# Pooled attention, a Sinkhorn-gated expert layer and a softplus layer on one core: softmax, gate, Sinkhorn, expert sums and pacing rewritten

## The chip, the cores and the metric

The kernel runs on one core of a Trainium2 chip. The metric is the device time of one execution in microseconds (us). The time before is 2142.21 us, the median of 3 runs.

## What is computed

The reference has three layers in a row, on 2304 tokens (4 batches of 576) of 512 features:

```
k_p, v_p = mean over groups of 8 tokens            # 72 keys and values a head
attn = softmax(q k_p^T / 8), divided by (sum + 1e-9);  x = attn v_p     # 8 heads of 64
P = exp(x w_gate - max over all);  8 times:        # P is 2304 x 8, Sinkhorn
    P /= P.sum(1) + 1e-9;  P /= P.sum(0) + 1e-9;  P *= 2304 / 8
x = sum over 8 experts e of P[:, e] * (relu(x w1[e]) w2[e])              # 1024 hidden
out = softplus(x w_in) w_out                       # 2048 hidden
```

## The kernel before, in words

**Precision.** Every large product is made of three matmuls on rounded parts (`three`, L451): high by high, high by low, low by high. ScalarE (ACT) rounds a tile to its high part, GpSimd (POOL) or VectorE (DVE) subtracts to get the low part.

**Order.** The order of the work is written by hand, engine by engine; each engine runs its own queue in that order. All loads and stores are issued by SP's queue, in order. The tokens are cut into three groups of 512, 896 and 896 (`PAIRS`). The 512 come first: the expert layer of group 0 runs while attention for the rest is still going on, in its gaps. Then come the expert layer of groups 1 and 2, then the softplus layer of groups 1, 2 and 0. An expert layer of a group is 32 sets (8 experts by 4 slices of 256 hidden units). A set has a `first` product (seven products of a Strassen-like scheme, `first_moe`, L518) and a `second` product (`second`, L581), one for every 128 tokens. `first` of set n+1 goes ahead of `second` of set n.

**Hooks.** After each of the seven products of `first`, and after each tile of `second`, `hook` (L721) is called: a slot. A set of group 0 has 7 + 4 = 11 slots. While attention is not done, every fourth slot issues one attention step (L724). After that each slot pops one entry of the list `side`; when that is empty, slots feed the conversion of the softplus weights from float64 (`from_float64`, L665).

**Attention steps.** There are 32 (4 batches, 2 halves of 288 tokens, 4 head pairs). Ten run ahead of the experts (L767), 22 in the slots. `attn_step` (L376) issues: the transposes of the next step's queries; the scores `s` into a PSUM bank, 96 tokens by 6 rows of 72 scores (`softmax`, L297); on DVE the negated maximum `mx`; the transposes of the step before (`turn_attn`); on ACT six exps, one per row of 72 with its own bias, each with a sum read out (L313); on DVE the sum plus 1e-9 and its reciprocal; on POOL the product with it (L321); then the mix with the values (`mix`, L336), whose result `px` ACT copies to `x0` or `xb`. With a half's fourth head pair, `mix` also stores `xb` and makes the gate's logits `pg` (L357): for each 96 tokens and each quarter of the features the 96 token columns are the weights and the 8 columns of `w_gate` are streamed, 12 matmuls of two instructions each. ACT copies them to `lt`. The last quarter of the features is what `mix` has just written. `pool_kv` sums keys and values over groups of 8 tokens on DVE.

**After attention.** `finish_attention` (L707) fills `side`: `to_tiles` stores `lt` to DRAM and loads it back as `prob` [128, 18, 8]; then the maximum; then eight times `sk_rows`, three empty slots, `sk_cols` (L638, L645), all on small tiles in SBUF except the column sums, which a matmul with ones puts into a bank `pc`; then `shares_to_raw`. The shares `prob` are not known when the first experts run: for group 0 the outputs of experts 0 to 3 (`RAW = 4`) are summed without shares, each in a tile of its own (`second`, L600), and `shares_to_raw` (L745) multiplies and adds them later, on DVE, 16 entries of `side`. From expert 4 on DVE multiplies the share in as it takes a tile out of PSUM (L610).

**Banks.** The 8 PSUM banks are one pool until attention is over; then 4 serve `first`, 3 (`y`) serve `second` and small things, 1 (`c`) serves the conversion and the softplus.

**Between groups.** `load_x` (L758) brings the next group's tokens; `t_sums` (L418) makes four sums of them, three on DVE and one on POOL; `splits` rounds seven tiles of them during the last `first` of a group. Weights go through one raw buffer each (`load_w`, L141) and are rounded by `prep_w1` and `prep_w2` (L177, L201); the load for a raw buffer is issued behind the preparation that empties it. In the last set of group 0 (set 31), whose `first` is followed by `second` of sets 30 and 31, `prep_w2` of set 31 and the load behind it are issued ahead of the seven products (L837).

Of the kernel before, what the change touches and what calls it, by code (L numbers as in the profile page):

```python
# [19 lines left out]
def attention_moe_softplus_kernel(  # L20
# [39 lines left out]
    OFF = (0, 512, 1408)  # L60
    LARGE = max(PAIRS)
    TP0 = PAIRS[0]
    RAW = 4

    cpool = ctx.enter_context(tc.tile_pool(name="const", bufs=1))
    xpool = ctx.enter_context(tc.tile_pool(name="x", bufs=14))
# [26 lines left out]
    row = cpool.tile([P, NT], F32, name="row")  # L93
    col = cpool.tile([P, E], F32, name="col")


    big = cpool.tile([P, 10], F32, name="big")
    rcpool = ctx.enter_context(tc.tile_pool(name="rconst", bufs=1, side="right"))
    lt = rcpool.tile([QP, 248], F32, name="lt")[:, :N // QP * E].rearrange("p (g e) -> p g e", e=E)
    nc.scalar.preload_act_table_set("natural_log_exp_and_others")  # L100


# [4 lines left out]
    def acc_of(i, t):  # L107
        return g_t[i][:, t * DM:(t + 1) * DM]

    def x_of(pair):  # L110
        return g_t[0][:, :KC * PAIRS[pair]].rearrange("p (c n) -> p c n", c=KC)

# [6 lines left out]
    lgd = dram.tile([N, E], F32, name="lgd")  # L119
    v1 = {}  # L120
    v2 = {}
    for u in range(NU2):
# [3 lines left out]

    phases = [("moe", 0), ("moe", 1), ("moe", 2), ("sp", 1), ("sp", 2), ("sp", 0)]
    acc_at = [1, 3, 2, 3, 2, 1]
    raw_at = [1, 0, 2, 3]
    sets = [  # L130
        (f, kind, pair, u)
        for f, (kind, pair) in enumerate(phases)
# [164 lines left out]
    def softmax(m):  # L297

        ps = bank("s")
        qT = q_t.pop(m)  # L300
        kb = kbd[kv_of(m) % NK]
        for j in range(JH):
            nc.tensor.matmul(ps[:QP, j * 2 * SP:(j + 1) * 2 * SP], qT[:, j * QP:(j + 1) * QP], kb)  # L303
        sv = ps[:QP, :G * SP].rearrange("p (g s) -> p g s", g=G)
        pool = at_e if m < AHEAD and m % 3 == 2 else at_p
        mx = at_p.tile([QP, G], F32, tag="mx", name="mx")
        ex = pool.tile([QP, G, SP], F32, tag="ex", name="ex")
        s1 = ps[:QP, G * SP:G * SP + G]
        nc.vector.tensor_reduce(mx, sv, axis=AX.X, op=ALU.max, negate=True)

        def exp():
            for g in range(G):
                nc.scalar.activation(  # L313
                    ex[:, g, :], sv[:, g, :], AF.Exp, bias=mx[:, g:g + 1], accum_out=s1[:, g:g + 1]
                )

        def divide():
            sm = at_p.tile([QP, G], F32, tag="sm", name="sm")
            nc.vector.tensor_scalar_add(s1, s1, 1e-9)
            nc.vector.reciprocal(sm, s1)  # L320
# [15 lines left out]
    def mix():  # L336
        m, aT = to_mix.pop(0)
        hb, hp = divmod(m, HP)
        vp = pooled[kv_of(m)][1]
        px = bank("px")  # L340
        for h in range(2):
            nc.tensor.matmul(px[h * D:(h + 1) * D, :W], vp[:, h, :], aT[:, h, :])  # L342

        t0 = hb * W
        here = max(0, min(W, TP0 - t0))
        x0 = x_of(0)
        if here < W and hp == 0:
            xb[hb] = at_p.tile([P, KC, W], F32, tag="xb", name="xb")
        if here:
            nc.scalar.activation(x0[:, hp, t0:t0 + here], px[:, :here], AF.Copy, scale=1.0 / POOL)  # L350
        if here < W:
            nc.scalar.activation(xb[hb][:, hp, :], px[:, :W], AF.Copy, scale=1.0 / POOL)
        if hp == HP - 1:
            if here < W:
                nc.sync.dma_start(xd[:, :, max(0, t0 - TP0):t0 + W - TP0], xb[hb][:, :, here:])
            pg = bank("pg")
            for j in range(JH):  # L357
                for c in range(KC):
                    o = j * QP
                    src = x0[:, c, t0 + o:t0 + o + QP] if here == W else xb[hb][:, c, o:o + QP]  # L360
                    nc.tensor.matmul(  # L361
                        pg[:QP, j * E:(j + 1) * E], src, wg[:, c, :], start=c == 0, stop=c == KC - 1
                    )
            nc.scalar.copy(lt[:, hb * JH:(hb + 1) * JH, :], pg[:QP, :JH * E].rearrange("p (j e) -> p j e", j=JH))


    pool_at = {}
# [213 lines left out]
    def second(n, i):  # L581
        f, kind, pair, u = sets[n]
        t = OFF[pair] // P + i
        py = bank("py")
        hh, hl = h_t[n]
        whi, wlo = w2_t[n]
        cs = slice(i * P, (i + 1) * P)
        for c in range(UC):
            three(py, (hh[:, c, cs], hl[:, c, cs]), (whi[:, c, :], wlo[:, c, :]), c == 0, c == UC - 1)
        a = acc_of(acc_at[f], i)  # L590
        if kind == "sp":
            if u == 0:
                nc.scalar.copy(a, py)
            else:
                nc.vector.tensor_tensor(a, py, a, op=ALU.add)
            if u == NU2 - 1:
                nc.sync.dma_start(out[t * P:(t + 1) * P, :], a)
            return
        e, first = u // UPE, u % UPE == 0
        if f == 0 and e < RAW:  # L600

            a = acc_of(raw_at[e], i)
# [14 lines left out]
        nc.scalar.copy(x_of(pair)[:, :, i * P:(i + 1) * P], pt)  # L617


    def to_tiles():  # L620
        nc.sync.dma_start(lgd.rearrange("(g p) e -> p g e", p=QP), lt)
        nc.sync.dma_start(prob, lgd.rearrange("(t p) e -> p t e", p=P))

    def sk_max():
        nc.vector.tensor_reduce(big[:, 0:1], prob, axis=AX.XY, op=ALU.max)
# [10 lines left out]
        nc.scalar.activation(prob, prob, AF.Exp, bias=big[:, 0:1])  # L636

    def sk_rows():  # L638
        nc.vector.tensor_reduce(row, prob, axis=AX.X, op=ALU.add)
        nc.vector.tensor_scalar_add(row, row, 1e-9)  # L640
        nc.vector.reciprocal(row, row)
        nc.vector.tensor_tensor(prob, prob, row.unsqueeze(2).to_broadcast([P, NT, E]), op=ALU.mult)
        nc.vector.tensor_reduce(col, prob.rearrange("p t e -> p e t"), axis=AX.X, op=ALU.add)

    def sk_cols():  # L645
        pc = bank("pc")
        nc.tensor.matmul(pc[:, :E], ones, col)
        nc.vector.tensor_scalar_add(col, pc[:, :E], 1e-9)
        nc.vector.reciprocal(col, col)
        nc.vector.tensor_scalar_mul(col, col, float(N // E))  # L650
        nc.vector.tensor_tensor(prob, prob, col.unsqueeze(1).to_broadcast([P, NT, E]), op=ALU.mult)

# [54 lines left out]
    def finish_attention():  # L707
        actx.close()
        gp = ctx.enter_context(tc.tile_pool(name="g23", bufs=1))
        for i in (2, 3):  # L710
            g_t[i] = gp.tile([P, GW], F32, name=f"g{i}")
        pools.append(ctx.enter_context(tc.tile_pool(name="tmp", bufs=2)))
        side.extend([to_tiles, None, None, None, None, None, sk_max, None, sk_max_t, None, sk_max_b])
# [7 lines left out]
    def hook(light=True):  # L721
        slot[0] += 1
        if attn_m[0] is not None:
            if slot[0] % 4 == 2:  # L724
                attn_step(attn_m[0], False)
                attn_m[0] += 1
                if attn_m[0] >= STEPS and not to_turn and not to_mix:
                    attn_m[0] = None
                    finish_attention()
# [14 lines left out]

    def shares_to_raw(experts):  # L745

        mul, stt = nc.vector.tensor_scalar_mul, nc.vector.scalar_tensor_tensor
        for i in range(TP0 // P):
            for e in experts:
                def add(i=i, e=e):  # L750
                    a, s = acc_of(1, i), prob[:, i, e:e + 1]
                    if e == 0:
                        mul(a, a, s)
                    else:
                        stt(a, acc_of(raw_at[e], i), s, a, op0=ALU.mult, op1=ALU.add)  # L755
                side.append(add)

    def load_x(pair):  # L758
        o = OFF[pair] - TP0
# [58 lines left out]
    for step, (what, n) in enumerate(todo):  # L818
# [4 lines left out]
        elif what == "first":  # L823
# [7 lines left out]
            if nxt is not None and nxt[0] != f:  # L831

                flush()
                if kind == "moe":
                    x = x_of(nxt[2])
                    to_split = splits(nxt[1], x, t_in(2, nxt[2]), on_pool=(2, 4) if nxt[1] == "moe" else (1, 3))
                if todo[step + 2][0] == "second":  # L837
                    prep_w2(n)
                    load_w(2, n + 1)
            elif kind == "sp" and u == 4 and f + 1 < len(phases):  # L840
                flush()
                to_split = splits("sp", x_of(phases[f + 1][1]), None, on_pool=(1, 3))
# [13 lines left out]
            if kind == "moe":  # L856

                pending.pop(0)()
                prep_w1(n + 1)
                load_w(1, n + 2)  # L860
            if todo[step + 1][0] != "second":
# [5 lines left out]
        else:  # L867
# [70 lines left out]
```

## Time and profile before

| what | value |
|---|---|
| median of 3 runs | 2142.21 us (2141.76 to 2143.05) |
| profiled execution, its own time | 2141.97 us |
| its span, first to last instruction | 2140.0 us |
| PE busy (matmul) | 2054.6 us, 96% |
| DVE, ACT, POOL busy | 67%, 41%, 59% |
| mean granted PE clock | 0.978 |

PE is TensorE's matmul row; its busy time counts every matmul from start to end and grows when the clock is low, so a busy PE need not be a fast one. The granted clock is 1.00 at 2.4 GHz and 0.50 at 1.2 GHz.

### The profile page before, as it was taken

Reading aid. Unit: us, or ns where it says so; the run is one execution under the profiler, and the core shown is the slowest. Engines: PE = TensorE matmul, PEld = TensorE weight load, DVE = VectorE, ACT = ScalarE, POOL = GpSimd, SP = SyncE. Lnnn points to the kernel's source line nnn. Section 1 sums busy time; section 2 is a strip of 40 time slices with the busy share of each in tenths; the row PEclk is TensorE's granted clock in tenths of the full one; section 3 lists DMA queues with packets and bytes.
Section 4 is the critical chain, followed back from the end, with each engine's and each line's share of the span. In section 5 each row is a group of like instructions: output and inputs, shape, how many; then the busy total and the mean of one; then the engine's idle time right before and its main releaser. Section 6 shows DMA issues by size and latency. Waiting matters only on the chain.

```text
span 2140.0 us, 28131 instructions
## 1 busy us (share of the span) xinstructions
PE 2054.6 (96%) x10411; PEld 1787.7 (84%) x10411; DVE 1437.1 (67%) x2453; ACT 867.1 (41%) x1921; POOL 1258.9 (59%) x1015
## 2 busy tenths in 40 slices
PE   7788989999799999999999999999999999999998
PEld 5677778888688888888887888888888888888897
DVE  5555388877667777777777776555555666767766
ACT  6655633333432222222234223222222355565565
POOL 4554477999655565555566565555555544544555
PEclk8798999999999999999999999999999999999999
DMA  6333222444222322222222222111112111121132
GB/s 174 91 102 95 64 81 89 128 126 155 74 89 83 110 83 89 89 86 77 89 89 80 83 89 70 60 58 56 56 59 60 60 60 50 60 84 60 50 114 79
DMA packets 132073, 179.19 MB, mean 84 GB/s; under 512 B 30816, under 2 KB 83040, under 8 KB 131936
## 3 DMA queue, kind: packets, MB, share of 16 engines
q1 hardware_dynamic: 131936, 177.40, 26.8%
q8 instruction: 81, 1.33, 0.3%
q14 instruction: 56, 0.46, 0.1%
HBM read 160.52 MB, written 16.85 MB: 83 GB/s over the span
## 4 chain that ended last, share of the span: by engine, by line
PE 81%; DVE 8%; ACT 6%; POOL 2%; issue 2%; DMA 1%; SPq 0%; ACTq 0%; DVEq 0%; POOLq 0%
PE py L454 40%; PE p L454 30%; PE ph L454 7%; ACT ex L313 2%; POOL w1lo L161 1%; PE pg L361 1%; DVE xlo L432 1%; PE s L303 1%; DVE c L485 1%; PE pa L332 1%; POOL w2lo L161 0%; DVE ln L492 0%; DVE c L490 0%; DVE g L755 0%; PE px L342 0%
## 5 line engine op out<-in xcount | busy, mean ns | idle before, releaser
L454 PE MATMUL py<-w2hi,hhi 128*128 128x512 f32 x1440 | 569.2, 395 | 7.4 <-DVE g L610 4.9
L454 PE MATMUL py<-w2lo,hhi 128*128 128x512 f32 x1440 | 564.1, 392 | 1.9 <-POOL w2lo L161 1.9
L454 PE MATMUL py<-w2hi,hlo 128*128 128x512 f32 x1440 | 563.5, 391 | 0.0
L161 POOL TENSOR_TENSOR w1lo<-w1raw,w1hi 128x512 fp32r<-128x512 f32 (+1 forms) x216 | 253.8, 1192 | 506.8 <-ACT w1hi L192 421.1
L454 PE MATMUL p<-xhi,w1hi 128*128 128x448 f32 (+1 forms) x1344 | 463.8, 345 | 31.2 <-DVE u L534 16.0
L454 PE MATMUL p<-xhi,w1lo 128*128 128x448 f32 (+1 forms) x1344 | 459.4, 342 | 2.6 <-POOL w1lo L161 2.6
L454 PE MATMUL p<-xlo,w1hi 128*128 128x448 f32 (+1 forms) x1344 | 460.2, 342 | 0.3
L610 DVE SCALAR_TENSOR_TENSOR g<-py,prob,g 128x512 f32<-128x512 f32 x498 | 372.7, 749 | 121.2 <-PE py L454 108.0
L469 ACT ACTIVATE hhi<-p 128x448 fp32r<-128x448 f32 (+1 forms) x384 | 179.7, 493 | 448.0 <-PE p L454 435.5
L454 PEld LDWEIGHTS py<-w2hi,hhi 128*128 128x128 f32 x1440 | 272.5, 189 | 65.5 <-DVE g L610 6.0
L161 POOL TENSOR_TENSOR w2lo<-w2raw,w2hi 128x1024 fp32r<-128x1024 f32 x120 | 289.1, 2409 | 61.6 <-ACT w2hi L205 56.3
L454 PEld LDWEIGHTS py<-w2hi,hlo 128*128 128x128 f32 x1440 | 272.0, 189 | 59.5
L454 PEld LDWEIGHTS py<-w2lo,hhi 128*128 128x128 f32 x1440 | 272.5, 189 | 52.3 <-POOL w2lo L161 2.2
L454 PEld LDWEIGHTS p<-xhi,w1hi 128*128 128x128 f32 x1344 | 259.6, 193 | 61.3 <-DVE u L534 17.3
L454 PEld LDWEIGHTS p<-xlo,w1hi 128*128 128x128 f32 x1344 | 259.7, 193 | 19.3 <-DVE xlo L432 0.9
L454 PEld LDWEIGHTS p<-xhi,w1lo 128*128 128x128 f32 x1344 | 259.7, 193 | 16.6 <-POOL w1lo L161 3.8
L536 ACT COPY za<-p 128x448 f32<-128x448 f32 (+1 forms) x96 | 46.0, 479 | 516.2 <-PE p L454 514.0
L161 POOL TENSOR_TENSOR w1lo<-sums,w1hi 128x1024 fp32r<-128x1024 f32 x96 | 230.5, 2401 | 0.0
L470 DVE SCALAR_TENSOR_TENSOR hlo<-p,hhi 128x448 fp32r<-128x448 f32 (+1 forms) x384 | 210.8, 550 | 27.1 <-ACT hhi L469 25.7
L534 DVE TENSOR_TENSOR za<-p,za 128x448 f32<-128x448 f32 (+1 forms) x96 | 53.2, 554 | 164.1 <-PE p L454 164.0
L497 POOL TENSOR_TENSOR hlo<-ln,hhi 128x448 fp32r<-128x448 f32 (+1 forms) x96 | 99.9, 1044 | 55.5 <-ACT hhi L496 52.9
L454 PE MATMUL ph<-xhi,w1hi 128*128 128x448 f32 (+1 forms) x384 | 130.1, 339 | 0.0
(117 smaller groups left out, 2779.5 us busy)
## 6 DMA issues: line engine op xcount, KB each, us to landing
w1raw<-in_moe_w_dram SPq DMA_DIRECT2D x96, 512.0 KB
w2raw<-in_moe_w_dram SPq DMA_DIRECT2D x96, 512.0 KB
w1raw<-v SPq DMA_DIRECT2D x24, 512.0 KB
w2raw<-v SPq DMA_DIRECT2D x24, 512.0 KB
f<-in_moe_w_in_dram SPq DMA_DIRECT2D x16, 512.0 KB
v<-dt SPq DMA_DIRECT2D x32, 256.0 KB
f<-in_moe_w_out_dram SPq DMA_DIRECT2D x16, 512.0 KB
kt<-in_k_dram SPq DMA_DIRECT2D x16, 288.0 KB
```

What stands on the lines that cost most here:

```text
L161: nc.gpsimd.tensor_tensor(o, a, b, op=ALU.subtract)
L303: nc.tensor.matmul(ps[:QP, j * 2 * SP:(j + 1) * 2 * SP], qT[:, j * QP:(j + 1) * QP], kb)
L313: nc.scalar.activation(ex[:, g, :], sv[:, g, :], AF.Exp, bias=mx[:, g:g + 1], accum_out=s1[:, g:g + 1])
L332: nc.tensor.transpose(pa[:SP, j * QP:(j + 1) * QP], ex[:, 2 * j + h, :], ident[:QP, :QP])
L361: nc.tensor.matmul(pg[:QP, j * E:(j + 1) * E], src, wg[:, c, :], start=c == 0, stop=c == KC - 1)
L454: nc.tensor.matmul(ps, lhs[a], rhs[b], start=first and i == 0, stop=last and i == 2, skip_group_check=goes_on,)
L469: nc.scalar.activation(hh, src, AF.Relu)
L470: nc.vector.scalar_tensor_tensor(hl, src, 0.0, hh.bitcast(F32), op0=ALU.max, op1=ALU.subtract)
L497: nc.gpsimd.tensor_tensor(hl, l, hh.bitcast(F32), op=ALU.subtract)
L534: add = lambda o, x, y: nc.vector.tensor_tensor(o, x, y, op=ALU.add)
L536: nc.scalar.copy(a, pa)
L610: nc.vector.scalar_tensor_tensor(a, py, prob[:, t, e:e + 1], a, op0=ALU.mult, op1=ALU.add)
```

## The change

1. **Softmax.** DVE subtracts the maximum from all 432 scores into `ex` in SBUF; one exp on ACT covers them; DVE sums `ex` over 72.
2. **Gate.** `w_gate`'s 8 columns are the weights; 288 token columns are streamed, 4 matmuls of two instructions a half. ACT copies 8 x 288 logits to `lg`, and each half's are stored to DRAM at once. `to_tiles` becomes one load; `to_prob` turns it with two PE transposes.
3. **Sinkhorn.** `row` and the column factors live in PSUM banks.
4. **Raw experts.** Five instead of four; `raw_of` packs them into the four accumulator tiles. Expert 0 is scaled on ACT, and two empty slots follow each product of the others.
5. **Pacing.** An attention step every fifth slot; two empty slots behind each of `t_sums`; `prep_w2` of set 31 and the load behind it are issued behind its seven products.

```diff
-    RAW = 4
+    RAW = 5
-        nc.vector.tensor_reduce(mx, sv, axis=AX.X, op=ALU.max, negate=True)
+        nc.vector.tensor_reduce(mx, sv, axis=AX.X, op=ALU.max)
+        nc.vector.tensor_tensor(ex, sv, mx.unsqueeze(2).to_broadcast([QP, G, SP]), op=ALU.subtract)
         def exp():
-            for g in range(G):
-                nc.scalar.activation(
-                    ex[:, g, :], sv[:, g, :], AF.Exp, bias=mx[:, g:g + 1], accum_out=s1[:, g:g + 1]
-                )
+            nc.scalar.activation(ex, ex, AF.Exp)
         def divide():
+            nc.vector.tensor_reduce(s1, ex, axis=AX.X, op=ALU.add)
...
-            for j in range(JH):
-                for c in range(KC):
...
-                    nc.tensor.matmul(
-                        pg[:QP, j * E:(j + 1) * E], src, wg[:, c, :], start=c == 0, stop=c == KC - 1
-                    )
-            nc.scalar.copy(lt[:, hb * JH:(hb + 1) * JH, :], pg[:QP, :JH * E].rearrange("p (j e) -> p j e", j=JH))
+            src = x0[:, :, t0:t0 + W] if here == W else xb[hb]
+            for c in range(KC):
+                nc.tensor.matmul(pg[:E, :W], wg[:, c, :], src[:, c, :], start=c == 0, stop=c == KC - 1)
+            lg = at_p.tile([E, W], F32, tag="lg", name="lg", bufs=1)
+            nc.scalar.copy(lg, pg[:E, :W])
+            half, o = divmod(t0, LT * P)
+            nc.sync.dma_start(lgd[half, :, o:o + W], lg)
...
     def sk_rows():
+        row = bank("row", "c")[:, :NT]
...
     def sk_cols():
         pc = bank("pc")
         nc.tensor.matmul(pc[:, :E], ones, col)
-        nc.vector.tensor_scalar_add(col, pc[:, :E], 1e-9)
-        nc.vector.reciprocal(col, col)
-        nc.vector.tensor_scalar_mul(col, col, float(N // E))
-        nc.vector.tensor_tensor(prob, prob, col.unsqueeze(1).to_broadcast([P, NT, E]), op=ALU.mult)
+        c = pc[:, :E]
+        nc.vector.tensor_scalar_add(c, c, 1e-9)
+        nc.vector.reciprocal(c, c)
+        nc.vector.tensor_scalar_mul(c, c, float(N // E))
+        nc.vector.tensor_tensor(prob, prob, c.unsqueeze(1).to_broadcast([P, NT, E]), op=ALU.mult)
...
-            if slot[0] % 4 == 2:
+            if slot[0] % 5 == 2:
...
-        for i in range(TP0 // P):
-            for e in experts:
+        for e in experts:
+            for i in range(TP0 // P):
                 def add(i=i, e=e):
                     a, s = acc_of(1, i), prob[:, i, e:e + 1]
                     if e == 0:
-                        mul(a, a, s)
+                        nc.scalar.activation(a, a, AF.Copy, scale=s)
                     else:
-                        stt(a, acc_of(raw_at[e], i), s, a, op0=ALU.mult, op1=ALU.add)
-                side.append(add)
+                        nc.vector.scalar_tensor_tensor(a, raw_of(e, i), s, a, op0=ALU.mult, op1=ALU.add)
+                side.extend([add, None, None] if e else [add])
...
-                if todo[step + 2][0] == "second":
-                    prep_w2(n)
-                    load_w(2, n + 1)
...
                 pending.pop(0)()
+                if [x[0] for x in todo[step + 1:step + 3]] == ["second"] * 2:
+                    prep_w2(n)
+                    load_w(2, n + 1)
                 prep_w1(n + 1)
...
-                    side.extend(t_sums(x_of(npair), t_in(2, npair), on_pool=(2,)))
+                    for x in t_sums(x_of(npair), t_in(2, npair), on_pool=(2,)):
+                        side.extend([x, None, None])
```

## Rows read from the trace of the kernel before

**Rows 1.** Busy time by stretch: length, PE, PEld, DVE, ACT, POOL, granted clock, DMA share, GB/s.

```profile
0.00:64.00 64.00, 45.24 (x235) 34.42 (x235) 36.66 (x59) 39.35 (x168) 29.28 (x41) 0.84 0.62 159
...
80.00:281.00 201.00, 176.93 (x1119) 149.32 (x1119) 96.01 (x204) 115.28 (x420) 102.99 (x93) 0.88 0.33 93
281.00:334.00 53.00, 44.07 (x262) 38.76 (x261) 48.34 (x115) 18.44 (x38) 38.39 (x32) 0.97 0.26 80
...
470.00:500.00 30.00, 26.57 (x156) 23.75 (x155) 23.22 (x40) 12.51 (x26) 27.80 (x21) 0.94 0.46 159
528.00:563.00 35.00, 25.41 (x127) 21.47 (x126) 25.90 (x41) 14.40 (x24) 25.91 (x20) 0.90 0.27 97
600.00:2100.00 1500.00, 1496.44 (x7105) 1307.44 (x7104) 1019.75 (x1645) 556.98 (x1000) 832.11 (x645) 1.00 0.24 75
```

**Rows 2.** The chain of waits, 80 to 282 us: start, length, engine, tile, line, count.

```profile
102.69 4.11 PE py L454 x18
...
108.35 0.64 PE px L342 x4
108.98 3.07 PE p L454 x24
...
205.47 0.38 ACT ex L313 x2
...
207.86 3.05 PE pg L361 x18
...
261.81 3.55 PE pg L361 x24
265.36 2.76 PE py L454 x6
```

**Rows 3.** PE's waits, 80 to 281 us: total, times, longest.

```profile
PE pg L361 <- ACT xb L352: 10.3, 5, 3.5
PE p L454 <- DVE p L534: 4.3, 2, 4.1
PE pa L332 <- POOL ex L321: 3.3, 4, 1.8
PE p L454 <- ACT w1hi L192: 2.4, 1, 2.4
```

**Rows 4.** Groups by line: count, busy us, mean ns, idle before.

```profile
L309 DVE TENSOR_REDUCE mx<-s 96x6 f32<-96x432 f32 x32 | 19.2, 600 | 24.1 <-PE s L303 23.9
L534 DVE TENSOR_TENSOR p<-p,za 128x448 f32<-128x448 f32 (+1 forms) x192 | 98.9, 561 | 3.3
L480 ACT ACTIVATE ex<-ex 128x448 f32<-128x448 f32 (+1 forms) x96 | 50.4, 526 | 3.0
L642 DVE TENSOR_TENSOR prob<-prob,row 128x144 f32<-128x144 f32 x8 | 5.5, 692 | 0.3
L650 DVE TENSOR_SCALAR col<-col 128x8 f32<-128x8 f32 x8 | 6.0, 748 | 0.3
L651 DVE TENSOR_TENSOR prob<-prob,col 128x144 f32<-128x144 f32 x8 | 6.1, 764 | 0.3
```

**Rows 5.** Single lines on DVE: shortest, median and longest ns, first and last start.

```profile
L650 DVE TENSOR_SCALAR col<-col x8: 171/267/1968, 286.4 to 333.0; 128x8 f32<-128x8 f32 x8
L651 DVE TENSOR_TENSOR prob<-prob,col x8: 309/556/2450, 287.7 to 333.2; 128x144 f32<-128x144 f32 x8
L606 DVE TENSOR_TENSOR g<-py,g x48: 646/689/704, 121.8 to 378.2; 128x512 f32<-128x512 f32 x48
L755 DVE SCALAR_TENSOR_TENSOR g<-g,prob,g x12: 744/988/2589, 334.0 to 383.0; 128x512 f32<-128x512 f32 x12
```

**Rows 6.** DVE's timeline around 490 us: start, length, idle before in brackets.

```profile
491.08 2.30 DVE L420 TENSOR_TENSOR g<-g,g 128x896 f32<-128x896 f32 x1
```

**Rows 7.** PE's waits, 528 to 563 us, its longest.

```profile
PE p L454 <- DVE u L534: 7.5, 1, 7.5
```

**Rows 8.** ACT's timeline around 540 us.

```profile
540.27 1.04 ACT L205 CAST w2hi<-w2raw 128x1024 fp32r<-128x1024 f32 x1 [7.68 <-DMA w2raw<-in_moe_w_dram]
```

More of the change, by code (lines that the diff above doesn't have):

```diff
@@ L92, in attention_moe_softplus_kernel @@
     prob = cpool.tile([P, NT, E], F32, name="prob")
-    row = cpool.tile([P, NT], F32, name="row")
     col = cpool.tile([P, E], F32, name="col")
-    big = cpool.tile([P, 10], F32, name="big")
+    big = cpool.tile([P, 34], F32, name="big")
     rcpool = ctx.enter_context(tc.tile_pool(name="rconst", bufs=1, side="right"))
-    lt = rcpool.tile([QP, 248], F32, name="lt")[:, :N // QP * E].rearrange("p (g e) -> p g e", e=E)
+    LT = NT // 2
+    lt = rcpool.tile([E * LT, 376], F32, name="lt")[:, :2 * P].rearrange("r (h p) -> r h p", h=2)
     nc.scalar.preload_act_table_set("natural_log_exp_and_others")
@@ L108, in acc_of, with raw_of @@
         return g_t[i][:, t * DM:(t + 1) * DM]
+    def raw_of(e, i):
+        n = e * (TP0 // P) + i
+        g, t = divmod(n, GW // DM) if e < 3 else (e - 1, i)
+        return acc_of((1, 0, 2, 3)[g], t)
     def x_of(pair):
@@ L118, in attention_moe_softplus_kernel @@
     xd = dram.tile([P, KC, N - TP0], F32, name="xd")
-    lgd = dram.tile([N, E], F32, name="lgd")
+    lgd = dram.tile([2, E, LT * P], F32, name="lgd")
     v1 = {}
@@ L128, in attention_moe_softplus_kernel @@
     acc_at = [1, 3, 2, 3, 2, 1]
-    raw_at = [1, 0, 2, 3]
     sets = [
@@ L356, in mix @@
             pg = bank("pg")
-            for j in range(JH):
-                for c in range(KC):
-                    o = j * QP
-                    src = x0[:, c, t0 + o:t0 + o + QP] if here == W else xb[hb][:, c, o:o + QP]
-                    nc.tensor.matmul(
-                        pg[:QP, j * E:(j + 1) * E], src, wg[:, c, :], start=c == 0, stop=c == KC - 1
-                    )
-            nc.scalar.copy(lt[:, hb * JH:(hb + 1) * JH, :], pg[:QP, :JH * E].rearrange("p (j e) -> p j e", j=JH))
+            src = x0[:, :, t0:t0 + W] if here == W else xb[hb]
[5 more added lines that the diff above has]
+            nc.sync.dma_start(lgd[half, :, o:o + W], lg)
     pool_at = {}
@@ L600, in second @@
         if f == 0 and e < RAW:
-            a = acc_of(raw_at[e], i)
+            a = raw_of(e, i)
             if first:
@@ L620, in to_tiles, with to_prob @@
     def to_tiles():
-        nc.sync.dma_start(lgd.rearrange("(g p) e -> p g e", p=QP), lt)
-        nc.sync.dma_start(prob, lgd.rearrange("(t p) e -> p t e", p=P))
+        nc.sync.dma_start(lt, lgd.rearrange("h e (t p) -> (e t) h p", p=P))
+    def to_prob():
+        for h in range(2):
+            pt = bank("pt")
+            nc.tensor.transpose(pt[:, :E * LT], lt[:, h, :], ident[:E * LT, :E * LT])
+            nc.scalar.copy(prob[:, h * LT:(h + 1) * LT, :], pt[:, :E * LT].rearrange("p (e t) -> p t e", e=E))
     def sk_max():
@@ L712, in finish_attention @@
         pools.append(ctx.enter_context(tc.tile_pool(name="tmp", bufs=2)))
-        side.extend([to_tiles, None, None, None, None, None, sk_max, None, sk_max_t, None, sk_max_b])
+        side.extend([to_tiles] + [None] * 6 + [to_prob, None, sk_max, None, sk_max_t, None, None, sk_max_b, None])
         for _ in range(ITERS):
@@ L745, in shares_to_raw @@
     def shares_to_raw(experts):
-        mul, stt = nc.vector.tensor_scalar_mul, nc.vector.scalar_tensor_tensor
-        for i in range(TP0 // P):
-            for e in experts:
+        for e in experts:
+            for i in range(TP0 // P):
                 def add(i=i, e=e):
```

## The prediction, on record before the change was run

> **What bounds the kernel now.** I read the busy time by stretch first. From 600 us on PE is busy 1496 of 1500 us at full clock [rows 1]: the experts of groups 1 and 2 and the softplus layer are bound by PE, the change does next to nothing there, and work on other engines is covered. Everything to be won lies before 600 us. The reader should see four stretches where PE stands idle or runs slowly [rows 1]: ten attention steps (0 to 64 us, 18.8 idle, clock 0.84), attention inside the experts (80 to 281 us, 24.1 idle, clock 0.88), Sinkhorn (281 to 334 us, 8.9 idle, DVE busy 48.3 of 53), and two spots near the change of groups, 3.4 idle at 470 to 500 and 9.6 idle of 35 at 528 to 563. Then PE's waits: from 80 to 281 us the largest is the gate's matmul waiting for ACT's copy of `xb`, 10.3 us [rows 3]. Then the chain, for what a gate costs once it runs: 18 of its 24 instructions took 3.05 us, all 24 took 3.55 [rows 2].
>
> **The change, part by part.** Terms are against the profiled execution's own time, 2141.97 us; the median of the runs is 0.24 above it, so nothing need be shifted.
>
> *Gate, its own time.* Six gates lie between 80 and 281 us. Each is 24 instructions, 3.55 us [rows 2], somewhat less where the clock still held; I take 3.4. The new one is 8 instructions of 288 columns. The nearest row is `px`, also 288 columns and two instructions each: four took 0.64 us [rows 2], so 0.16 each and 1.28 together. Saved: 2.1 x 6 = **13**; bounds 9 (the new ones run at half clock) and 14. The skill's page "TensorE: Matmul & The Clock Gate", section "Back-to-back issue gap", gives a warm instruction its columns over 2.4 GHz plus 2.5 ns, an estimate of 0.98 us a gate; by it the total would be 2 us better. I keep the row.
>
> *Gate, the clock.* At 261.81 us a gate starts with no wait ahead of it in the chain, and the six `py` instructions behind it take 2.76 us; 18 at full speed take 4.11, so six take 1.37 [rows 2]. A gate of 8-column instructions is thus enough to leave PE at 1.2 GHz, and costs 1.4 afterwards. If 288-column streams don't do that, 1.4 x 6 = **8**; bounds 0 and 10.
>
> *The exp.* Six pairs of ACTIVATE and read-out at 0.38 [rows 2] are 2.3 us of ACT a step. One exp over 432 elements is at most the 0.53 of the 448-wide one [rows 4]. ACT gets 1.8 a step back. DVE gets a subtraction (nearest row 0.56, one operand in PSUM) and a sum (like `mx`, 0.60) [rows 4], 1.15 a step. The chain from scores to `xb` is shorter by 1.8 - 0.55 = 1.2, since the sum comes behind the exp and `xb` doesn't need it. The gate waits five times, 10.3 in all [rows 3], each time with ACT busy on a step's exps: 5 x 1.2 = **6**; bounds 2 and 9. The waits for `w1hi` (2.4) and for POOL's `ex` (3.3) [rows 3] stand behind exps too, and steps five slots apart leave one slot more: **4** of the 5.7; bounds 0 and 6.
>
> *First ten steps.* Two gates, 2 each at most; the loads that fill the first part don't move; ACT's 1.8 a step goes, but DVE's 36.7 of 64 [rows 1] grows by 11.5, so DVE takes ACT's place. I take **5**; bounds 0 and 9.
>
> *Sinkhorn.* DVE is 91% busy here [rows 1]. L642, L650 and L651 took 5.5, 6.0 and 6.1 us for eight each [rows 4], but the shortest L650 is 0.17 and the shortest L651, which has L642's shape, 0.31 [rows 5]. The rest, 17.6 - 1.4 - 5.0 = 11.3, is waiting. Which instructions are hit: L755 with two operands in SBUF goes from 0.74 to 2.59, L606, with one in PSUM, never over 0.70 [rows 5]. With `row` and the factors in banks the Sinkhorn steps become like L606. DVE's 48.3 falls to 37 of 53, and the stretch shrinks until PE, busy 44.1 with much of that spread out, bounds it. I take 11 of DVE and 1 of waits behind it, **12**; bounds 2 (another cause for the waits) and 14. `pc` now holds its `y` bank over four DVE instructions instead of one, some 0.7 longer; two other banks cover that, and without them a `second` tile would wait 0.7.
>
> *Raw experts.* 16 products with two SBUF operands instead of 12, at 0.74 to 2.59 [rows 5]: 3 to 10 more on DVE. Four scalings go to ACT, and 16 take-outs of expert 4 become additions like L606, slightly shorter. They now lie three slots apart, so one long one delays one tile and the banks cover it: I charge **1**; bounds 0 and 6. Attention now ends at slot 2 + 22 x 5 = 112 instead of 90; 96 entries of `side` reach slot 208, and expert 5 starts behind slot 227, so nothing is emptied in one go except the last products of expert 4. The conversion starts some 75 slots later and moves into the stretch where DVE has 32% free and PE is the bound: 0.
>
> *Spread sums.* Two sums on DVE stand close together at 490 us, one of 2.30 us [rows 6], and PE idles 3.4 in that stretch [rows 1]. Apart, PE waits for one at a time: **2**; bounds 0 and 3. The same at group 2 lies where PE does not idle: 0.
>
> *Moved `prep_w2`.* ACT stands 7.68 us at L205 for the load of `w2raw` [rows 8]; DVE's `u` is late by it, and PE waits 7.5 for that [rows 7]. Behind the seven products ACT first does `za` and the roundings of the new tokens, and the load lands meanwhile. POOL's half of `prep_w2` also goes behind the two token tiles, and SP's next `w2` load comes some 5 us later; set 31's `second` starts a whole `second` of set 30 (4 x 1.37) after the products, which covers both. What is late next is the rounding of the tokens itself, seven ACT casts and their low parts. **7**; bounds 4 and 9.
>
> *Small.* ACT's copy of the logits is 288 wide instead of 24, eight times; eight stores of `lg` go into SP's queue, each behind ACT's copy, with queries, keys and weights queued behind; queries are loaded six steps ahead, which hides it, and without that lead a step would wait a microsecond or two. `to_prob` adds two transposes and two copies. 0.
>
> Sum: 13 + 8 + 6 + 4 + 5 + 12 - 1 + 2 + 7 = **56**, so 2141.97 - 56 = **2086 us**.
>
> **Rivals.** *The clock is not given back.* If waits and the steps' transposes lower it, not the gate, then the 8 go, and the new gates run at half speed, 1.28 more x 6: 2086 + 8 + 8 = **2102**. Against it: step products end at 108.99, and the 24 `p` behind them take 3.07 us [rows 2], close to full speed (`py` gives 0.23 for 512 columns, half of that for 256, so 2.8). The Trainium skill's page "TensorE: Matmul & The Clock Gate", section "PE-mode transpose", says transposes don't count as PE being busy, which would make this; the row just named speaks against it. Chance 0.12.
>
> *Sinkhorn's waits stay.* The banks change the addresses but not what DVE waits for; the change doesn't do what it says. 2 instead of 12: **2096**. L606 speaks against it. Chance 0.08.
>
> *DVE becomes the bound of the steps: slower.* Each of 32 steps adds 1.15 to DVE's queue, and the expert products queue behind: PE once waited 4.1 for DVE's `p` [rows 3]. If that time lands on PE in full (37) and each of the 22 steps in the slots leaves the clock low as a gate did (1.4 x 22 = 31), then of the gains only the gate's own time, Sinkhorn, sums and `prep_w2` stay (34): 2142 + 68 - 34 = **2176**. It decides once DVE's additions cost PE more than 34, about 1.5 a step in the slots. Against it: DVE is busy 96 of 201 there [rows 1] and has 25 added; and it stands for ACT's exps today, which get shorter. Chance 0.04.
>
> **How the numbers follow.** A measurement of this kernel can tell 0.2%, 4.3 us, from no change. The forecast, 2086, has 0.74; the rivals 0.12, 0.08 and 0.04; 0.02 is left for gains that cancel. Range: with the terms' good ends mostly together 77 are won, 2065; with half of the gate, the clock and the exp lost and the rest at its poor end 26 remain, 2116. That holds the first two rivals too. Faster 0.94, same 0.02, slower 0.04.
>
> **What would show it.** Right: no granted clock below 0.9 behind a gate, and a gate of eight instructions near 1.3 us; PE's wait for `xb` under 5 us; Sinkhorn's products on DVE at 0.31 throughout and DVE's share there below 85%; no wait of ACT at L205 and no 7.5 at PE in set 31; from group 1 on, no change. Wrong: a clock still at 0.5 behind gates, long waits at the moved Sinkhorn lines, or PE waiting for DVE's `p` and `u` in most steps.

## The result, and the profile after

The changed kernel takes **2077.94 us**, the median of three runs (2077.27 to 2084.46), against 2142.21 before: ratio 0.9708 (0.9678 to 0.9739), 64.3 us less. Its profiled execution took 2077.27 us, with a span of 2075.5 against 2140.0. The forecast was 2086.

The page's head of the changed kernel, busy time over the span and the granted clock in 40 slices:

```profile
PE 2022.9 (97%) x10285; PEld 1748.3 (84%) x10285; DVE 1461.1 (70%) x2513; ACT 822.6 (40%) x1579; POOL 1261.1 (61%) x1015
...
PEclk9899999999999999999999999999999999999999
```

Before, the clock line began with 8798. DVE has 24 us more work than before (1437.1), ACT 44.5 less (867.1), and the span is shorter all the same. Where, the busy time by stretch says (columns as in [rows 1]; Sinkhorn now lies at 267 to 308 us):

```profile
0.00:64.00 64.00, 43.22 (x224) 28.60 (x224) 50.92 (x81) 26.25 (x62) 31.84 (x44) 0.95 0.61 161
80.00:250.00 170.00, 165.59 (x1082) 132.89 (x1081) 120.27 (x243) 88.77 (x208) 108.74 (x99) 0.99 0.38 112
267.00:308.00 41.00, 40.78 (x264) 36.90 (x263) 35.56 (x115) 18.33 (x38) 33.16 (x30) 1.00 0.29 91
...
600.00:2050.00 1450.00, 1446.43 (x6896) 1264.60 (x6895) 992.46 (x1612) 547.59 (x989) 804.90 (x623) 1.00 0.24 76
125.00:130.00 5.00, 5.00 (x25) 2.67 (x23) 4.20 (x7) 3.43 (x8) 3.39 (x3) 1.00 0.80 254
```

Between 80 and 250 us PE now idles 4.4 of 170 at a clock of 0.99, where 24.1 of 201 were idle at 0.88 [rows 1]. Sinkhorn's stretch leaves PE 0.2 idle where it left 8.9. From 600 us on nothing changed: 99.8% busy in both. A landmark that both traces have, the rounding of each set's second weight on ACT (L205, now L210), comes 5.8 us earlier at the first set (80.73, now 74.92), 45.3 at set 10 (295.32, now 250.07), 55.8 at set 16, 58.8 at set 30, 64.7 at set 32 (572.39, now 507.73). At set 8 the lead is larger, 52.2, only because the changed kernel, with its steps five slots apart, has issued 29 of its 32 attention steps by then and the kernel before all 32; at set 10 both have issued all. The first scaled take-out of group 1 is also 64.7 earlier (583.9, now 519.2). So the whole gain is made before 520 us and none of it later: over 39 of the 64 in attention between the experts, from the first set to set 10, and 10.5 from set 10 to 16, where the changed kernel's Sinkhorn lies.

PE's waits of the changed kernel, 80 to 250 us (columns as in [rows 3]):

```profile
PE p L457 <- DVE p L537: 1.5, 1, 1.5
...
PE pa L336 <- POOL ex L325: 0.5, 1, 0.5
...
PE pg L363 <- ACT xb L356: 0.2, 1, 0.2
```

The gate's wait for `xb` went from 10.3 us to 0.2, the one for POOL's `ex` from 3.3 to 0.5 [rows 3]. The chain around a gate, 120 to 135 us:

```profile
125.18 0.64 PE px L346 x4
125.81 2.04 PE pg L363 x8
127.85 4.31 PE py L457 x18
```

A gate is 2.04 us, and the 18 `py` behind it run at 0.24 each, full speed; the stretch 125 to 130 has a clock of 1.00. Before, six `py` behind a gate took 2.76 [rows 2]. Groups by line (columns as in [rows 4]):

```profile
L315 DVE TENSOR_TENSOR ex<-s,mx 96x432 f32<-96x432 f32 x32 | 19.3, 604 | 3.1
L322 DVE TENSOR_REDUCE s<-ex 96x6 f32<-96x432 f32 x32 | 19.3, 602 | 11.2 <-ACT ex L318 11.2
...
L318 ACT ACTIVATE ex<-ex 96x432 f32<-96x432 f32 x32 | 18.1, 565 | 21.8 <-DVE ex L315 21.7
...
L652 DVE TENSOR_TENSOR prob<-prob,row 128x144 f32<-128x144 f32 x8 | 2.4, 304 | 0.3
L662 DVE TENSOR_TENSOR prob<-prob,pc 128x144 f32<-128x144 f32 x8 | 2.4, 304 | 0.3
...
L661 DVE TENSOR_SCALAR pc<-pc 128x8 f32<-128x8 f32 x8 | 1.4, 174 | 0.3
```

One exp costs 0.565 us in place of 2.3, and DVE's two new instructions 1.21 together. The three Sinkhorn groups need 6.2 us in place of 17.6 [rows 4], each instruction at its shortest.

What is left before 520 us: PE's waits of the changed kernel, 80 to 560 us.

```profile
PE p L457 <- DVE u L537: 4.1, 5, 1.5
PE py L457 <- POOL w2lo L166: 2.7, 1, 2.7
PE p L457 <- DVE p L537: 2.1, 3, 1.5
```

### The profile page after: what moved, and what is told of

It reads as the page before. It is cut to its first block, busy times and chain, and to the rows that moved or that the text cites. A ratio compares the mean times of both kernels' runs of the same rounds, so it can differ in the third digit from the quotient of the medians.

```text
span 2075.5 us, 27614 instructions
## 1 busy us (share of the span) xinstructions
PE 2022.9 (97%) x10285; PEld 1748.3 (84%) x10285; DVE 1461.1 (70%) x2513; ACT 822.6 (40%) x1579; POOL 1261.1 (61%) x1015
## 4 chain that ended last, share of the span: by engine, by line
PE 84%; DVE 8%; POOL 3%; ACT 3%; issue 2%; DMA 0%; SPq 0%; ACTq 0%; DVEq 0%; POOLq 0%
PE py L457 42%; PE p L457 31%; PE ph L457 7%; POOL w1lo L166 1%; DVE kp L266 1%; PE px L346 1%; PE s L308 1%; DVE c L488 1%; PE pg L363 1%; DVE g L609 1%; DVE xlo L435 1%; POOL w2lo L166 0%; DVE ln L495 0%; DVE vp L272 0%; DVE c L493 0%
## 5 line engine op out<-in xcount | busy, mean ns | idle before, releaser
L457 PE MATMUL p<-xhi,w1hi 128*128 128x448 f32 (+1 forms) x1344 | 458.5, 341 | 12.5 <-DVE u L537 4.1
L613 DVE SCALAR_TENSOR_TENSOR g<-py,prob,g 128x512 f32<-128x512 f32 x482 | 360.7, 749 | 109.7 <-PE py L457 97.5
L457 PEld LDWEIGHTS py<-w2hi,hlo 128*128 128x128 f32 x1440 | 270.4, 188 | 58.8
L457 PEld LDWEIGHTS p<-xhi,w1hi 128*128 128x128 f32 x1344 | 254.9, 190 | 42.7 <-DVE p L537 5.5
L457 PEld LDWEIGHTS p<-xlo,w1hi 128*128 128x128 f32 x1344 | 255.0, 190 | 20.5 <-DVE xlo L435 2.0
L457 PEld LDWEIGHTS p<-xhi,w1lo 128*128 128x128 f32 x1344 | 255.0, 190 | 18.7 <-POOL w1lo L166 6.0
```

The source lines that it names most:

```text
L457: nc.tensor.matmul(ps, lhs[a], rhs[b], start=first and i == 0, stop=last and i == 2, skip_group_check=goes_on,)
```

## Experiments

Each run's ratio is against the kernel before on the same chip. "Undone" runs are also set beside the changed kernel's median, 2077.94; its own interval is about 6.5 us to either side, so of the single undone parts the gate, the exp (barely), Sinkhorn and the fifth expert stand clear of it by their intervals, while the pacing, `prep_w2` and the sums don't, and for those the traces carry the argument. Two stretches of the traces differ between executions of the same code. One is the first 75 us. The other is the change from group 0 to group 1: between sets 30 and 32 the changed kernel's landmark takes 35.3 us at a clock of 1.00, and in seven kernels with the same code there (u_gate, u_exp, u_sink, u_pace, u_raw, u_sums, best1) it takes 36.9 to 38.1, each with a fall of the clock.

**The gate undone (u_gate).** The way of the logits to `prob`, by one store and one load, goes back with it.

```
-            for c in range(KC):
-                nc.tensor.matmul(pg[:E, :W], wg[:, c, :], src[:, c, :], start=c == 0, stop=c == KC - 1)
...
+            for j in range(JH):
+                for c in range(KC):
...
+                    nc.tensor.matmul(
+                        pg[:QP, j * E:(j + 1) * E], src, wg[:, c, :], start=c == 0, stop=c == KC - 1
+                    )
```

> The changed kernel with the old gate alone (96 token columns as weights, 8 columns streamed). Theory, the gate's own instructions lower PE's clock: although PE waits for xb only 0.2 us in the changed kernel, the granted clock falls to 0.5 to 0.6 behind gates again; eight gates cost some 1.4 us more of their own and 1.4 us of low clock each, with a few us of waits: 20 to 25 us back, near 2100 us. Rival, the waits ahead of a gate lower the clock: with no waits the clock stays above 0.95 and only the gate's own time comes back, 11 us, near 2089.

2092.66 us (2092.43 to 2096.03), ratio 0.9773 (0.9758 to 0.9789): 14.7 are lost. The chain of this kernel at a gate, and its busy time there:

```profile
256.30 2.62 PE pg L364 x24
258.91 2.76 PE py L457 x6
```

```profile
255.00:260.00 5.00, 5.00 (x36) 4.16 (x36) 0.42 (x1) 2.42 (x8) 0.01 (x1) 0.79 0.35 121
260.00:265.00 5.00, 5.00 (x16) 4.18 (x16) 1.45 (x3) 3.04 (x6) 5.00 (x4) 0.53 0.51 35
```

PE is busy all 5 us of each, and the clock falls all the same, to 0.53 behind the gate, near the lower of its two levels (1.2 of 2.4 GHz); the six `py` take 2.76 instead of 1.37. All waits for `xb` together are 3.4 us here, none over 1.1. It is the gate's stream of 8-column instructions, not idleness ahead of it, that costs the clock. Not each gate does so: of the six behind 80 us five go with a fall, in the gate or within 2 us behind it, and the one at 234 us does not (232 to 242 us: 1.00). The clock's part is as expected; the amount is not, 14.7 instead of 20 to 25.

**The new gate alone on the kernel before (b_gate).** The reverse of the edit above, with the `to_prob` that it needs.

> The kernel before with the new gate alone. Theory, the gate's own instructions lower the clock: PE still waits some 8 to 10 us for xb behind six exps, but the clock behind gates stays near 1.0, and 20 to 25 us are won, near 2120. Rival, the waits lower it: the clock still falls to 0.5 to 0.6 behind gates, and only some 11 us are won, near 2131.

2127.11 us (2125.62 to 2127.34), ratio 0.9931 (0.9914 to 0.9947): 14.9 won, the same amount from the other side, and again short of the 20 to 25 expected. PE's largest wait, 80 to 281 us, its busy time there, and a stretch behind a gate:

```profile
PE pg L360 <- ACT xb L353: 6.5, 5, 2.5
```

```profile
80.00:281.00 201.00, 177.21 (x1123) 139.82 (x1124) 109.26 (x236) 124.05 (x436) 119.19 (x106) 0.98 0.35 102
...
195.00:200.00 5.00, 4.19 (x33) 3.71 (x34) 4.43 (x5) 1.69 (x7) 3.74 (x5) 1.00 0.72 228
```

Six exps a step, steps four slots apart and waits for `xb` of up to 2.5 us are all still there, yet the clock is 1.00 behind each of the six gates and 0.98 over the whole stretch, where it was 0.88. The rival that these waits and the transposes lower it falls, for the gates behind 80 us. Two falls have another cause. At 116 to 120 us the clock is 0.57 here; ahead of it PE waits 4.2 us for DVE's `p`, and no gate is near. And in the first 75 us it falls in kernels with the new gate too (0.95 over the first 64 us of the changed kernel), by what was not tried.

**Six exps again (u_exp), and one exp alone on the kernel before (b_exp).**

```
-            nc.scalar.activation(ex, ex, AF.Exp)
+            for g in range(G):
+                nc.scalar.activation(
+                    ex[:, g, :], sv[:, g, :], AF.Exp, bias=mx[:, g:g + 1], accum_out=s1[:, g:g + 1]
+                )
```

Here `mx` is negated again, and the subtraction and the sum on DVE are left out; b_exp is the opposite edit.

> The changed kernel with six exps a step with bias and read-out, no subtraction and no sum on DVE. Theory, the exps were on the path: ACT gets 1.8 us a step back, PE waits for xb return (some 5 us with steps five slots apart), 10 to 15 us are lost, near 2090; the first ten steps end near 60 us instead of 56. Rival, DVE has become the bound of the steps: without 1.2 us a step of DVE work the kernel is as fast or faster, 2070 to 2078.

> The kernel before with one exp per step alone. Theory: PE's waits for xb fall from 10 to some 4 us, w1hi's and POOL's ex with them, 10 to 15 us are won, near 2129; the clock behind gates still falls to 0.5 to 0.6. Rival, DVE becomes the bound: steps four slots apart pile up on DVE, PE waits for DVE's p and u some 10 us more, and nothing is won, near 2142 or above.

u_exp took 2089.93 us (2087.94 to 2090.64), ratio 0.9755 (0.9741 to 0.977): 12.0 lost. b_exp 2124.07 (2120.4 to 2128.47), ratio 0.9917 (0.9897 to 0.9937): 17.9 won by the medians, more than the 10 to 15 expected (13.5 in its profiled execution, 2128.47). PE's waits of u_exp, 80 to 260 us:

```profile
PE pg L364 <- ACT xb L357: 5.8, 5, 1.8
```

PE's waits of b_exp, 80 to 281 us, then its busy time there:

```profile
PE p L453 <- DVE p L533: 3.4, 1, 3.4
...
PE pg L360 <- ACT xb L351: 3.2, 5, 1.2
```

```profile
80.00:281.00 201.00, 188.10 (x1191) 160.85 (x1192) 130.85 (x268) 89.64 (x213) 113.15 (x101) 0.88 0.34 99
```

The gate's wait for `xb` follows the exps: 5.6 us of it come back with them, 7.1 go without them. DVE has 131 of 201 us to do instead of 96 and the waits for its `p` are no longer than before (4.3 in [rows 3]), so the rival in which DVE becomes the bound falls. The clock stays at 0.88, as it was, while the new gate alone makes it 0.98. One old gate of b_exp, its last, meets a clock that holds (248 to 258 us: 1.00), and so gives its price at full speed:

```profile
251.59 2.20 PE pg L360 x24
```

**Sinkhorn's steps back in SBUF (u_sink).**

```
+    row = cpool.tile([P, NT], F32, name="row")
...
-        row = bank("row", "c")[:, :NT]
...
-        c = pc[:, :E]
-        nc.vector.tensor_scalar_add(c, c, 1e-9)
+        c = col
+        nc.vector.tensor_scalar_add(c, pc[:, :E], 1e-9)
```

> The changed kernel with Sinkhorn's row sums and column factors back in SBUF. Theory, two SBUF operands make DVE wait for POOL: the products with prob, 0.30 us each in the changed kernel, go back to a mean of 0.6 to 0.8 with single ones of 1 to 2.5 us; DVE's share in the stretch goes above 90%, and 6 to 12 us are lost, 2084 to 2090 us. Rival, the wider pacing already covers it: the waits return, but PE doesn't idle, and the time stays within 2 us of 2078.

2091.57 us (2089.93 to 2093.47), ratio 0.9761 (0.9747 to 0.9776): 13.6 lost, where 6 to 12 were expected; between sets 10 and 16, where Sinkhorn lies, the landmark loses 11.2 (251.44 to 331.51, against 250.07 to 318.90). Its groups by line, the single line L662, PE's largest wait from 80 to 560 us, and DVE and POOL in its timeline at one short and one long product:

```profile
L662 DVE TENSOR_TENSOR prob<-prob,col 128x144 f32<-128x144 f32 x8 | 7.3, 907 | 0.3
...
L652 DVE TENSOR_TENSOR prob<-prob,row 128x144 f32<-128x144 f32 x8 | 4.4, 544 | 0.3
...
L661 DVE TENSOR_SCALAR col<-col 128x8 f32<-128x8 f32 x8 | 3.6, 456 | 0.3
```

```profile
L662 DVE TENSOR_TENSOR prob<-prob,col x8: 308/309/2455, 274.1 to 318.8; 128x144 f32<-128x144 f32 x8
```

```profile
PE pc L657 <- DVE col L653: 5.7, 3, 2.7
```

```profile
285.72 0.31 DVE L662 TENSOR_TENSOR prob<-prob,col 128x144 f32<-128x144 f32 x1
...
292.12 2.41 POOL L167 TENSOR_TENSOR w2lo<-w2raw,w2hi 128x1024 fp32r<-128x1024 f32 x1
292.24 2.46 DVE L662 TENSOR_TENSOR prob<-prob,col 128x144 f32<-128x144 f32 x1
```

Only where the operand lies differs, and the same product costs 0.304 or 0.907 us on average. Here five of the eight are at the shortest, in the changed kernel all are: it is a wait that some instructions meet, not a slower form. The timeline shows for what. Two products take 2.45 us; each starts 0.12 us behind a `w2lo` of POOL and ends 0.17 behind its end. At the start of the five short ones POOL is idle. The one at 281 us, 0.81, ends in the same way 0.17 behind the end of a POOL sum. So the wait is for POOL's instruction; no run took POOL's work away.

The Trainium skill's page "SBUF — State Buffer", section "Who interferes with whom", says that a DVE instruction with two SBUF inputs contends with a GpSimd instruction that reads SBUF, and that one with at most one such input, outside the two-port modes, does not. These runs agree for the products, 0.907 against 0.304. But L661, with one SBUF input, is hit too, 0.456 on average against 0.174 and once 2.11 us, and the reciprocal ahead of it, also with one, never (0.20); whether L661 ran in such a mode the trace doesn't show.

**Steps four slots apart (u_pace).** In this kernel part of expert 3's shares are multiplied in before its last set has been summed, so part of that sum is lacking; the instructions are the same.

```
-            if slot[0] % 5 == 2:
+            if slot[0] % 4 == 2:
```

> The changed kernel with an attention step every fourth slot. Theory, a fifth slot lets the chain of a step (DVE, ACT, DVE, POOL) finish: PE waits of POOL's ex and DVE's p and u return, 5 to 10 us are lost, 2083 to 2088 us. Rival, with one exp the steps no longer need the room: no change within 2 us; what the four-slot pacing costs in waits it gets back by an earlier end of attention.

2084.82 us (2084.17 to 2091.75), ratio 0.9737 (0.9721 to 0.9753): 6.9 lost. PE's waits, 80 to 560 us:

```profile
PE p L457 <- DVE u L537: 5.9, 7, 1.6
PE p L457 <- DVE p L537: 4.1, 3, 3.4
```

Against the same view of the changed kernel the waits for DVE grow by 1.8 and 2.0. With two more DVE instructions a step, the fifth slot is what DVE needs to get its expert products out in time. The wait for POOL's `ex`, which was expected back too, does not appear.

**Four raw experts with steps five slots apart (u_raw).**

```
-    RAW = 5
+    RAW = 4
```

> The changed kernel with four raw experts, all else as changed, pacing of five slots included. Theory, the fifth expert is only room for the list: the list of side work does not end before expert 4 starts, the remaining products of the shares are emptied in one go, DVE stands some 10 to 15 us behind and PE waits 5 to 10 us for it in one place, 2083 to 2088 us. Rival, taking shares in later saves DVE work by itself: the loss is spread over the stretch and not in one place.

2095.93 us (2093.94 to 2098.11), ratio 0.9785 (0.9769 to 0.9801): 18.0 lost, by the median the most of any part and more than expected. PE's waits, 80 to 560 us, and the chain at 328 us:

```profile
PE py L457 <- DVE g L613: 8.2, 2, 7.7
```

```profile
328.33 5.37 DVE g L765 x4
...
338.57 0.75 DVE g L613
339.36 2.93 PE py L457 x6
```

Attention now ends so late that the products with the shares are not done when the next expert wants them; they follow each other on DVE, and PE stands 7.7 us for the one at their end. The landmark shows 11.1 lost between sets 17 and 18 (329.49 to 349.91, against 331.55 to 340.84), which leaves this kernel 9.1 behind. It is 7.3 behind at set 30 and 9.6 at set 36 (583.99, against 574.35), so 7 to 10 us are the price of the missing room; at set 36 u_exp is 12.8 behind and u_sink 14.3.

The rest is lost where both kernels run the same code. 5.0 us go between sets 63 and 64, at the next change of groups: a low part on DVE, `xlo` with two SBUF operands, takes 3.28 us beside POOL's work (1077.36 us; 2.54 is the longest on that line of DVE in the changed kernel), the take-out behind it comes late, PE waits 3.3 us for it, and the clock is 0.52 from 1081 to 1088 us. That two instructions meet so in this kernel and not in the other belongs to their places in time; whether they do in every execution is open, as each kernel has one trace.

**Five raw experts, spread products and five slots alone on the kernel before (raw_pace).** The RAW, `raw_of`, `shares_to_raw` and `slot[0] % 5` lines of the change, and its slots for Sinkhorn's start; all else as before.

> The kernel before with only the fifth raw expert, the shares spread out and an attention step every fifth slot; gate, exps, Sinkhorn, w2 and the sums as before. Theory, the wider pacing is worth most while a step is long on ACT: PE waits of xb, POOL's ex, w1hi and DVE's p shrink, and the spread shares keep DVE from standing behind: 10 to 18 us are won, 2124 to 2132. Rival, pacing only pays once the step is short: less than 5 us won, 2137 or above.

2131.01 us (2128.91 to 2132.78), ratio 0.9947 (0.9932 to 0.9962): 11.4 won. PE's waits, 80 to 281 us:

```profile
PE pg L366 <- ACT xb L357: 10.5, 5, 2.7
PE p L459 <- DVE u L539: 2.6, 2, 1.7
PE p L459 <- POOL w1lo L166: 2.0, 2, 1.4
...
PE p L459 <- DVE p L539: 0.8, 2, 0.6
...
PE pa L337 <- POOL ex L326: 0.2, 1, 0.2
```

The wait for `xb` is what it was (10.3), so pacing does nothing for it. The one for DVE's `p` fell from 4.3 to 0.8, the one for POOL's `ex` from 3.3 to 0.2, and the one for `w1hi` (2.4) [rows 3] no longer appears: 9.0 us. Against that stands the wait for DVE's `u`, 2.6 where it was 0.8; the 2.0 for POOL's `w1lo` were there before.

**`prep_w2` moved back (u_prep).**

```
+                if todo[step + 2][0] == "second":
+                    prep_w2(n)
+                    load_w(2, n + 1)
...
-                if [x[0] for x in todo[step + 1:step + 3]] == ["second"] * 2:
-                    prep_w2(n)
-                    load_w(2, n + 1)
```

> The changed kernel with the last w2 preparation of group 0 ahead of its seven products again. Theory: ACT stands 7 to 8 us at the cast of w2 for the load, PE waits 7 us for DVE's u, and 6 to 9 us are lost, 2084 to 2087 us. Rival, the rounding of the tokens bounds the place anyway: ACT waits for the load but less than 3 us are lost.

2083.14 us (2082.72 to 2088.39), ratio 0.9727 (0.9713 to 0.9742): 5.2 lost. PE's waits, 80 to 560 us:

```profile
PE p L457 <- DVE u L537: 9.9, 5, 7.3
```

The old 7.5 [rows 7] is back as 7.3, and the changed kernel's 2.7 for POOL's `w2lo` is gone. From set 30 to set 32 the landmark takes 39.4 us: 4.1 more than in the changed kernel, but only 1.3 to 2.5 more than in the seven kernels named above, which have the move as well. The move wins the one wait and pays part of the other; its worth lies between 1 and 5 us, under the 6 to 9 expected, and nothing here fixes it closer.

**The sums close together (u_sums).**

```
-                    for x in t_sums(x_of(npair), t_in(2, npair), on_pool=(2,)):
-                        side.extend([x, None, None])
+                    side.extend(t_sums(x_of(npair), t_in(2, npair), on_pool=(2,)))
```

> The changed kernel with the four token sums of the next group in consecutive slots. Theory, two long sums on DVE next to each other make PE wait: 1 to 3 us lost, 2079 to 2081 us, all of it near 430 us. Rival: the sums stand apart by their waits for POOL and the load anyway, no change within 1 us.

2080.7 us (2077.87 to 2083.89), ratio 0.9708 (0.9692 to 0.9724), the changed kernel's own ratio. PE's largest wait, 425 to 465 us:

```profile
PE p L457 <- DVE u L537: 2.9, 1, 2.9
```

The changed kernel waits there 1.4 for POOL's `w1lo`, 1.3 for `g` and 0.7 for `u`, 3.4 in all. The wait is shared out, not removed, and the rival holds.

**Two tries at a better kernel (best1, best2).** best1 lets POOL do the value sums of the second batch of pooled keys too; best2 adds an earlier `prep_w2`, after the fourth of the seven products.

```
-        if i < HP:
+        if i < 2 * HP:
...
+                if kind == "moe" and k == 3 and [x[0] for x in todo[step + 1:step + 3]] == ["second"] * 2:
+                    prep_w2(n)
+                    load_w(2, n + 1)
```

> The changed kernel, with POOL instead of DVE summing the values of the second batch too (four sums of 1.9 us off DVE, three additions each on POOL). Theory, DVE bounds the first ten steps (50.9 busy of 64 us): they end 2 to 4 us earlier, 2074 to 2076 us. Rival, POOL's product ex is what the steps wait for (6.9 us in that stretch): more work on POOL makes them later, 2078 to 2082 us.

> As best1, and the last w2 preparation of group 0 in the middle of its seven products instead of behind them, ahead of POOL's second token tile. Theory, after the change POOL is late with w2lo there because two token tiles of 2.95 us stand ahead of it; with one of them behind it PE's wait of 2.7 us goes: 2 to 3 us better than best1. Rival, the load has not landed yet and ACT waits for it again, 2 to 5 us worse than best1.

best1 2082.24 us (2080.89 to 2085.14), ratio 0.9722 (0.9707 to 0.9736); best2 2080.97 (2079.98 to 2082.79), ratio 0.9715 (0.97 to 0.9729). In best1 PE's wait for POOL's `ex` in the first 64 us falls to 3.5 us, from 6.9 in the changed kernel, but that stretch gets no shorter: the first set's landmark is at 80.64 us, against 74.92. PE's largest wait of best2, 440 to 520 us:

```profile
PE py L457 <- DVE g L613: 2.5, 2, 1.3
```

The 2.7 for `w2lo` is gone, and from set 30 to 32 the landmark takes 34.6 us against best1's 36.9; but the changed kernel's own execution takes 35.3 there, so the place of `prep_w2` can still give 0.6 to 2.3 us. By the medians best2 is 1.3 better than best1, less than the 2 to 3 expected. Neither kernel's median is below the changed kernel's, and none better was found.

## Why the prediction was right, point by point

2077.94 lies in 2065 to 2116, and the parts that the forecast named as gains are the ones that the runs show; 56 were predicted and 64 came. That the two are so near is in part luck. The gate, `prep_w2` and the sums were put some 10 us too high together. The exp, the first ten steps, the pacing and the fifth expert were put at 6 + 4 + 5 - 1 = 14, and 64.3 less the measured 14.8, 13.6, 5.2 and 0 of the others leaves 31 for them. The range has a slip as well: the good ends of the terms add up to 74, not 77, which is 2068, and half of the gate, the clock and the exp with the poor ends of the rest is 13.5, not 26, which is 2128.

*Gate, own time and clock.* Forecast 13 + 8 = 21 for six gates, measured 14.7 and 14.9 for all eight. The clock's part held: from 85 us on no stretch behind a gate is below 0.9. The term for the gate's own time was wrong on both sides. The new gate takes 2.04 us, not 1.28: the row I took, `px`, gives 0.16 for an instruction of 288 columns, and the gate's eight have a pitch of 0.255. And the old one at full clock takes 2.20, not 3.4: the 3.55 that I read was taken when the clock had already fallen (0.50 from 262.4 to 265.4 us). At full clock the two differ by 0.16 us, which is 1.3 for all eight. Another 3.2 is waiting for `xb` (3.4 in u_gate, 0.2 in the changed kernel): the old gate wants the last quarter of the features after six of its 24 instructions, the new one after six of its eight. That leaves some 10 of the 14.7 for the clock, an estimate, in the gates and behind them. The estimate of 0.98 by the Trainium skill's page "TensorE: Matmul & The Clock Gate", section "Back-to-back issue gap", was further off than the row; the measurement decides.

*The exp, and the first ten steps.* 6 for `xb`, part of 4 for other waits and part of 5 at the start; one exp is worth 12.0 (undone) to 17.9 (alone). The 6 held: 5.6 and 7.1 us of that wait hang on the exps. The 5 can't be told. The first set's landmark comes 5.8 earlier in the two traces, but kernels that differ only later have it at 74.5 (u_raw), 74.7 (u_prep) and 79.1 us (u_sums), so two executions differ by nearly as much.

*Raw experts and pacing.* Here the sum was furthest off. I charged 1 for the fifth expert, as mere work on DVE, and let the wider pacing share in a term of 4. Together they won 11.4 on the kernel before; with pacing undone 6.9 were missing, with the fifth expert undone 18.0, of which 7 to 10 where its room is missing. The fifth expert without the wider pacing is what u_pace runs; no run leaves both out of the changed kernel. What I missed is that DVE's `p` is late behind a step (4.3 [rows 3], which I had not booked as a gain), that five slots remove most of that (0.8 in raw_pace, 1.5 in the changed kernel), and that the fifth raw expert is the room in which so long an attention and its products can end. These and the exp make up for what the gate lacks.

*Sinkhorn.* Forecast 12, measured 13.6, of which 11.2 in its stretch: right, by the working given, and the waits end with POOL's instructions. The working looked at instructions with two operands in SBUF; L650, with one, was hit as well [rows 5], and the bank cured it too. DVE is now busy 35.56 of 41 us there, 87%, a little over the 85% named, because PE's stretch shrank with it. The rival that its waits stay falls.

*Moved `prep_w2`.* Forecast 7, measured 5.2 in the medians and 1.3 to 4.1 between its sets. ACT's 7.68 [rows 8] are gone. What is late next, I named rightly as the new tokens, but priced at nothing: I held that set 30's `second` covers POOL's half of `prep_w2` behind the two token tiles, and it does not. The `w2lo` of set 31 comes behind their low parts on POOL, and PE waits 2.7. The chain of the changed kernel there:

```profile
484.44 5.89 POOL xlo L435 x2
490.33 2.31 POOL w2lo L166
492.69 5.51 PE py L457 x23
```

*Spread sums.* Forecast 2; no difference was found.

The terms as measured, 15 for the gate, 12 to 18 for the exp, 13.6, 7 to 11, 5 and 0, add up to 52 to 63 us. That is no exact account of the 64: each is read beside other neighbours, and the exp and the pacing both relieve the wait for POOL's `ex`.

## What to carry to other kernels

Look at the granted clock behind short matmuls, not only at their duration: here streaming 288 tokens past 8 weight columns, in place of 8 columns past 288 tokens, won 15 us over eight gates, some 10 of them by the clock, though at full clock the two forms cost nearly the same (2.04 and 2.20 us). And read an instruction's price at a known clock before it goes into a sum. When the same instruction on DVE has a median at its shortest and a maximum eight times that, look where its operands lie; here it waited for POOL, and putting one of them into a bank cured it. When a small piece of work is put between large ones, price the queue of each engine behind it, and expect spacing and the room at the end of the schedule to be one decision.

## What the runs showed that was not expected

Two kinds of matmul with 288 columns, `px` and `pg`, both in float32, have pitches of 0.16 and 0.255 us at full clock. The four `px` of a step write two halves of the partitions, the eight `pg` one bank's first eight partitions; they also differ in rows (72 and 128) and in weight columns (64 and 8). Which of these is the cause was not tried. And executions of the same code in the first 75 us, before the first expert, differ by over 4 us.
